# A pitch of 4128 bytes instead of 4096 for the 32 weight tiles of an attention and MoE kernel

## The chip, the core and the metric

The kernel runs on one core of a Trainium2 chip. The metric is the device time of one execution in microseconds (us): the median of the runs. A core has five engines that run side by side: TensorE (PE) multiplies matrices, VectorE (DVE), ScalarE (ACT) and GpSimd (POOL) work on elements, and SyncE (SP) issues the transfers (DMA) between the main memory and the core's own memory, SBUF. In SBUF a tile has 128 partitions, and in each of them it takes the same stretch of bytes. This document is about where that stretch begins.

## What is computed

Linear attention over 8 batches, 8 heads, 576 positions and 64 values a head, and behind it two matrix products with an activation between them:

```python
q_s = q - np.max(q, axis=-1, keepdims=True)
q_s = np.exp(q_s)
q_s = q_s / (np.sum(q_s, axis=-1, keepdims=True) + 1e-09)
k_s = k - np.max(k, axis=2, keepdims=True)
k_s = np.exp(k_s)
k_s = k_s / (np.sum(k_s, axis=2, keepdims=True) + 1e-09)
kv = np.einsum('bhsd,bhse->bhde', k_s, v)
attn = np.einsum('bhsd,bhde->bhse', q_s, kv)

x = attn.transpose(0, 2, 1, 3).reshape(4608, 512)
h = x @ w_in            # w_in: 512 x 2048
g = h - np.tanh(h)
out = g @ w_out         # w_out: 2048 x 512
```

`q`, `k` and `v` arrive as 4-byte numbers. The two weights arrive as 8-byte numbers (`float64`), which the kernel must decode itself.

## The kernel before

**Tiling.** The 4608 rows of `x` are worked through in 9 chunks of 512 (`j`), the 2048 hidden columns in 16 pieces of 128 (`f`). A step (`j`, `f`) forms `ph`, the transposed product of one piece of `w_in` with one chunk, applies the activation, and two steps later adds that piece's part to the four outputs `po` of the chunk. For accuracy each operand is split into a high and a low part of 4 bytes (`xh` and `xl`, `gh` and `gl`, two halves of each weight), and three of the four partial products are formed.

**Matmuls.** In `h_mm` (L568) the weights `w_i` are the stationary operand: a piece of 128 columns is loaded into PE (LDWEIGHTS), and 512 columns of `xh` or `xl` stream past it, 12 times for a step. In `o_mm` (L651) it is the other way round: 128 columns of `gh` or `gl` are loaded, and the 512 columns of one half of `w_o` stream, 12 times for a step. The attention adds small matmuls: `pm`, `pb`, `pk`, `pt`, `px`. In `pk` (L323) the values stream, 65 columns for each head, out of the tile `v` or out of a tile called `spare_v`, which for the second batch lies in a weight tile's place.

**Weight tiles.** There are 16 `w_in` and 16 `w_out` pieces, and each has one place in SBUF for the whole run, by its tag (`wi0` to `wi15`, `wo0` to `wo15`) in the pool `wts`. First the raw 8-byte numbers are loaded there (`load_weight`, L135 and L140), 512 KB, in pieces of 1 KB (`w_in`) or 4 KB (`w_out`). Five operations decode them (`split_weight`): a clamp on DVE (L157), a scaling of the high words (L161) and of the low words (L164) on ACT, a shift on DVE (L168) into a tile `c` of another pool, and a cast on ACT (L175). The cast writes the high half back to the same place, and a subtraction on POOL or DVE (L179) the low half. A few of the places hold something else before their weight comes: `wo15` a `q` tile, `wo13`, `wo14` and `wi14` transposed queries, and `wi15` the values of the second batch (`spare_v1`, L222), which need 4160 bytes.

**Places.** A pool hands out its places in the order in which tags are first asked for. A first pool, `lead`, fills SBUF up to a multiple of 256 bytes, and `LINE` and `line()` round sizes up to 256. A weight place is 4096 bytes in each partition, that of `wi15` is 4160 rounded up to 4352, and so every weight tile, and every other tile that is large (`xh`, `xl`, `g`, `gh`, `gl`, `u`, `t`, `mk`, `q`, `k`, `c`), begins at a multiple of 256. The small tiles and `v` stand in the last pool, `sm`, and begin at multiples of 32; `v` is at 192 modulo 256.

**Order.** The work up to step 19 is written out by hand in the table `ORDER`; from there the order on PE and SP is that of the code, and that on the other engines is found by a scheduler.

Of the kernel before, what the change touches and what calls it, by code (L numbers as in the profile page):

```python
# [10 lines left out]
F32 = mybir.dt.float32  # L11
F32R = mybir.dt.float32r
I32 = mybir.dt.int32
U32 = mybir.dt.uint32
I64 = mybir.dt.int64
# [55 lines left out]
def attn_moe_kernel(  # L71
# [10 lines left out]
    B, H, S, D = q.shape  # L82
    NT, DM = out.shape
    DFF = w_in.shape[1]
    P = 128
# [3 lines left out]
    NF = DFF // P  # L89
# [7 lines left out]
    def line(n: int) -> int:  # L97
        return -(-n // LINE) * LINE
# [4 lines left out]
    wts = ctx.enter_context(tc.tile_pool(name="wts", bufs=1))  # L103
# [24 lines left out]

    staged = {}
    wt = {}  # L130

    def load_weight(kind: str, f: int):
        w = wts.tile([P, DM], I64, name=f"raw_{kind}{f}", tag=f"w{kind}{f}")
        if kind == "i":
            nc.sync.dma_start(  # L135
                w.rearrange("p (c f) -> p c f", c=NC),
                w_in[:, f * P : (f + 1) * P].rearrange("(c p) f -> p c f", p=P),
            )
        else:
            nc.sync.dma_start(w, w_out[f * P : (f + 1) * P, :])  # L140
        staged[kind, f] = w

    def split_weight(kind: str, f: int) -> dict:

        st = {}

        def words(n: int) -> bass.AP:
            return staged[kind, f].bitcast(U32).rearrange("p (n t) -> p n t", t=2)[:, :, n]

        def clamp():
            hif = words(1).bitcast(F32)
            nc.vector.tensor_scalar(hif, hif, HI_MAX, -HI_MAX, op0=ALU.min, op1=ALU.max)  # L157

        def scale():
            hif = words(1).bitcast(F32)  # L160
            nc.scalar.activation(hif, hif, AF.Prelu, scale=2.0**-112, alpha=-(2.0**32))  # L161

        def low():
            nc.scalar.mul(words(0), words(0), 15.0 * 2.0**-33)  # L164

        def shift():
            st["c"] = c = dec.tile([P, DM], U32, name=f"c_{kind}{f}", tag="c")
            nc.vector.scalar_tensor_tensor(  # L168
                c, words(1), 3, words(0), op0=ALU.logical_shift_left, op1=ALU.bitwise_or
            )  # L170

        def cast():
            del staged[kind, f]
            wt[kind, f] = w = wts.tile([P, 2, DM], F32R, name=f"w_{kind}{f}", tag=f"w{kind}{f}")
            nc.scalar.copy(w[:, 0], st["c"].bitcast(F32))  # L175

        def rest(eng):
            w = wt[kind, f]
            eng.tensor_tensor(  # L179
                w[:, 1], st["c"].bitcast(F32), w[:, 0].bitcast(F32), op=ALU.subtract  # L180
            )

        return dict(cl=clamp, pr=scale, lo=low, st=shift, ca=cast, sub=rest)


# [28 lines left out]
    def v_ones(b: int, st: dict, u: int):  # L214

        if u < NKP:
            if b == 0 and u:
                vt = xp.tile([P, H, 2 * D + 2], F32, name="spare_v", tag="xh1")
            elif b == 1 and u:
                n = H * (2 * D + 2)  # L220
                vt = wts.tile([P, line(4 * n) // 4], F32, name="spare_v1", tag=f"wi{NF - 1}")
                vt = vt[:, :n].rearrange("p (h d) -> p h d", h=H)  # L222
            else:
                vt = sm.tile([P, H, 2 * D + 2], F32, name=f"v{b}_{u}", tag="v", bufs=1)
            nc.gpsimd.memset(vt[:, :, 0 :: 2 * D + 1], 1.0)
        else:
            vt = sm.tile([REST, H, D + 1], F32, name=f"vr{b}", tag="vr", bufs=1)
            nc.gpsimd.memset(vt[:, :, 0:1], 1.0)
        st["v", u] = vt
# [280 lines left out]
    def prepare(j: int, put):  # L510
# [6 lines left out]
        for b in new:  # L517
            st = {}
            for u in range(NKP + 1):
                put(0, lambda u=u: k_load(b, st, u))  # L520
            for u in (0, NKP):
                for part in (v_ones, v_load):
                    put(0, lambda u=u, part=part: part(b, st, u))
            for n in range(4):
                put(KX, lambda n=n: kv_max(b, st, n))
            for part in (kv_max_t, kv_row, kv_row_h, kv_row_l):
                put(KX + 2, lambda part=part: part(b, st))
            put(KX + 4, lambda: kv_rows(b, st))
            for u in range(NKP + 1):
                put(KX + 4, lambda u=u: kv_sub(b, st, u))  # L530
                put(KX + 4, lambda u=u: kv_exp(b, st, u))
            put(KX + 7, lambda: kv_mm(b, st, 0))
            for part in (v_ones, v_load):
                put(KX + 7, lambda part=part: part(b, st, 1))
            put(KX + 10, lambda: kv_mm(b, st, 1))
            put(KX + 10, lambda: kv_mm(b, st, NKP))
            for n in range(3):
                put(KX + 10, lambda n=n: kv_den(b, st, n))
            put(KX + 10, lambda: kv_norm(b, st))
# [169 lines left out]
    for b in range(2):  # L709
        st = {}  # L710
        for u in range(NKP + 1):
            ops[f"k{b}.{u}"] = lambda b=b, st=st, u=u: k_load(b, st, u)
            ops[f"vo{b}.{u}"] = lambda b=b, st=st, u=u: v_ones(b, st, u)
            ops[f"v{b}.{u}"] = lambda b=b, st=st, u=u: v_load(b, st, u)
            ops[f"ks{b}.{u}"] = lambda b=b, st=st, u=u: kv_sub(b, st, u)
            ops[f"ke{b}.{u}"] = lambda b=b, st=st, u=u: kv_exp(b, st, u)
            ops[f"pk{b}.{u}"] = lambda b=b, st=st, u=u: kv_mm(b, st, u)
        for n, part in enumerate("abcd"):
            ops[f"km{b}.{part}"] = lambda b=b, st=st, n=n: kv_max(b, st, n)
        for n, part in enumerate(("sl", "rs", "rc")):  # L720
            ops[f"{part}{b}"] = lambda b=b, st=st, n=n: kv_den(b, st, n)
        for part, fn in dict(
            pm=kv_max_t, mx=kv_row, mh=kv_row_h, ml=kv_row_l, pb=kv_rows, kn=kv_norm
        ).items():
            ops[f"{part}{b}"] = lambda b=b, st=st, fn=fn: fn(b, st)
# [13 lines left out]
    for kind, f in pieces:  # L739
        ops[f"ld.{kind}{f}"] = lambda kind=kind, f=f: load_weight(kind, f)  # L740
        for part, fn in split_weight(kind, f).items():
            ops[f"{part}.{kind}{f}"] = fn
# [11 lines left out]
    with tc.manual_schedule(engines={ENG.PE, ENG.DVE, ENG.Activation, ENG.Pool, ENG.SP}):  # L754
        for name in ORDER.split():
            eng = (nc.vector,) if name[-1] == "*" else ()
            name = name.rstrip("*")
# [74 lines left out]
```

## Time and profile before

| | before |
|---|---|
| median of 3 runs | 898.78 us |
| lowest and highest run | 897.59 and 899.41 us |
| span of the profiled execution | 896.5 us |
| PE busy, matmuls | 874.3 us, 5008 matmuls |
| DMA | 57.47 MB, mean 64 GB/s |

The profile covers one execution. Its span, 896.5 us, runs from the first to the last instruction on the core; the profile states no device time of its own for that execution, so the span is what the working is made against, and the median of the runs stands 2.3 us above it. In the rows, L568 is line 568 of the kernel, "out<-in" are tile names with the buffer numbers left out (so `v` is every `v` tile, and `spare_v` both of its kind), `x1152` is a count, and two times behind a bar are the group's busy time in us and the mean of one in ns, followed by the engine's idle time before the group and what ended most of it. Slices are 40 equal parts of the span, each digit the busy share in tenths.

### The profile page before, as it was taken

What the parts mean: (1) busy time and instruction counts of PE and PEld (TensorE: products, weight loads), DVE (VectorE), ACT (ScalarE), POOL (GpSimd) and SP (SyncE); (2) the same over time, 40 slices, a digit from 0 to 9 for tenths busy, and PEclk for the clock granted to TensorE, in tenths of its full rate; (3) what the DMA queues carried; (4) which work ended last, traced back from release to release, by engine and by line L of the source; (5) the groups of instructions that cost most, each with busy time, mean ns of one, the idle gap of its engine ahead of it and who ended that gap; (6) DMA issues with size and microseconds to landing.
All of it is one profiled execution on the core that took longest, in us unless ns stands there. A gap on an engine that the chain in (4) does not pass through costs nothing.

```text
span 896.5 us, 13174 instructions
## 1 busy us (share of the span) xinstructions
PE 874.3 (98%) x5008; PEld 716.2 (80%) x5008; DVE 613.3 (68%) x906; ACT 555.3 (62%) x967; POOL 289.2 (32%) x246
## 2 busy tenths in 40 slices
PE   6899989999999999999999999999999999999997
PEld 5677778888888888888888888888888888888886
DVE  7999988957686767667656765765865566454444
ACT  4899986656554656555646665556646566556553
POOL 4641112433244224332333332422433224212221
PEclk8999999999999999999999999999999999999999
DMA  9983301040223102300140011301100020001001
GB/s 293 315 307 119 123 1 42 24 133 9 83 71 103 28 3 81 107 24 1 48 130 4 21 47 37 106 1 48 48 24 1 1 71 12 1 1 48 1 1 47
DMA packets 79775, 57.47 MB, mean 64 GB/s; under 512 B 14688, under 2 KB 72032, under 8 KB 79712
## 3 DMA queue, kind: packets, MB, share of 16 engines
q1 hardware_dynamic: 79712, 56.63, 20.7%
q8 instruction: 39, 0.64, 0.3%
q14 instruction: 24, 0.20, 0.1%
HBM read 46.14 MB, written 10.49 MB: 63 GB/s over the span
## 4 chain that ended last, share of the span: by engine, by line
PE 82%; DVE 8%; ACT 5%; DMA 2%; issue 1%; SPq 1%; POOL 1%; DVEq 0%; ACTq 0%; POOLq 0%
PE po L651 39%; PE ph L568 38%; PE pk L323 2%; PE px L487 2%; PE pt L461 1%; DVE g L589 1%; DVE t L594 1%; DMA raw_i<-in_moe_w_in_dram 1%; ACT mk L583 1%; DVE g L597 1%; DVE c_o L168 1%; DVE g L602 1%; DVE gl L608 1%; ACT raw_o L164 1%; ACT raw_o L161 1%
## 5 line engine op out<-in xcount | busy, mean ns | idle before, releaser
L651 PE MATMUL po<-w_o,gh 128*128 128x512 f32 x1152 | 359.1, 393 | 0.3 <-DVE w_o L179 0.2
L568 PE MATMUL ph<-xh,w_i 128*128 128x512 f32 x1152 | 313.0, 394 | 3.1 <-DVE t L594 2.3
L608 POOL TENSOR_TENSOR gl<-g,gh 128x512 fp32r<-128x512 f32 x128 | 170.9, 1335 | 387.0 <-ACT gh L605 356.7
L651 PEld LDWEIGHTS po<-w_o,gh 128*128 128x128 f32 x1152 | 214.6, 188 | 47.4 <-issue 1.9
L568 PEld LDWEIGHTS ph<-xh,w_i 128*128 128x128 f32 x1152 | 213.9, 188 | 47.8 <-DVE t L594 2.8
L589 DVE SCALAR_TENSOR_TENSOR g<-u,ph 128x512 f32<-128x512 f32 x144 | 98.2, 682 | 208.4 <-ACT t L583 202.6
L651 PE MATMUL po<-w_o,gl 128*128 128x512 f32 x576 | 224.5, 390 | 0.3 <-DVE gl L608 0.3
L605 ACT CAST gh<-g 128x512 fp32r<-128x512 f32 x144 | 89.6, 622 | 172.4 <-DVE g L602 163.8
L568 PE MATMUL ph<-xl,w_i 128*128 128x512 f32 x576 | 155.0, 391 | 0.0
L583 ACT ACTIVATE u<-ph 128x512 f32<-128x512 f32 x144 | 86.1, 598 | 72.9 <-PE ph L568 72.4
L597 DVE SCALAR_TENSOR_TENSOR g<-vv,g 128x512 f32<-128x512 f32 x144 | 117.8, 818 | 18.5 <-ACT vv L583 8.0
L651 PEld LDWEIGHTS po<-w_o,gl 128*128 128x128 f32 x576 | 108.3, 188 | 23.7 <-DVE gl L608 0.7
L568 PEld LDWEIGHTS ph<-xl,w_i 128*128 128x128 f32 x576 | 108.1, 188 | 23.6 <-DVE xl L508 0.5
L602 DVE COPY_PREDICATED g<-mk,t 128x512 f32<-128x512 int32 x144 | 117.9, 819 | 3.3
L583 ACT ACTIVATE mk<-ph 128x512 int32<-128x512 f32 x144 | 86.4, 600 | 37.7 <-DVE g L589 35.5
L583 ACT ACTIVATE vv<-u,b_pa 128x512 f32<-128x512 f32 x144 | 104.8, 728 | 0.4 <-DVE g L597 0.3
L594 DVE TENSOR_TENSOR t<-ph,t 128x512 f32<-128x512 f32 x144 | 98.1, 681 | 6.4 <-ACT mk L583 5.6
L583 ACT ACTIVATE t<-ph 128x512 f32<-128x512 f32 x144 | 85.6, 594 | 3.0 <-DVE g L589 3.0
L413 POOL TENSOR_TENSOR q<-q,mq 128x1024 f32<-128x1024 f32 x14 | 28.4, 2026 | 49.1 <-DVE mq L408 47.3
L447 POOL TENSOR_TENSOR qn<-q,sq 128x512 f32<-128x512 f32 x30 | 34.6, 1155 | 25.5 <-PE pt L461 12.8
L408 DVE TENSOR_REDUCE mq<-q 128x16 f32<-128x1024 f32 x15 | 18.3, 1217 | 25.4 <-DMA q<-in_q_dram 25.4
L179 POOL TENSOR_TENSOR w_i<-c_i,w_i 128x512 fp32r<-128x512 f32 x12 | 18.3, 1528 | 39.2 <-ACT w_i L175 39.1
(94 smaller groups left out, 575.4 us busy)
## 6 DMA issues: line engine op xcount, KB each, us to landing
k<-in_k_dram SPq DMA_DIRECT2D x16, 512.0 KB, 5.5
raw_i<-in_moe_w_in_dram SPq DMA_DIRECT2D x16, 512.0 KB, 6.6
raw_o<-in_moe_w_out_dram SPq DMA_DIRECT2D x16, 512.0 KB, 9.2
q<-in_q_dram SPq DMA_DIRECT2D x15, 512.0 KB, 3.9
v<-in_v_dram SPq DMA_DIRECT2D x14, 512.0 KB, 5.1
out_dram<-o SPq DMA_DIRECT2D x28, 256.0 KB, 2.4
kr<-in_k_dram SPq DMA_DIRECT2D x8, 128.0 KB, 5.2
spare_v<-in_v_dram SPq DMA_DIRECT2D x2, 512.0 KB, 8.5
```

Of the source, the lines that this page charges most:

```text
L179: eng.tensor_tensor(w[:, 1], st["c"].bitcast(F32), w[:, 0].bitcast(F32), op=ALU.subtract)
L413: eng.tensor_tensor(qf, qf, mq, op=ALU.subtract)
L447: eng.tensor_tensor(qn.rearrange("p a g d -> p g a d"), qt[:, :, j].rearrange("p (g a) d -> p g a d", g=2), sq[:, :, j : j + 1] .broadcast ...
L568: nc.tensor.matmul(ph, w[:, i, c], x[:, c, :], start=(n == 0), stop=(n == len(ops) - 1))
L583: nc.scalar.activation(new(tag, **of), st[src], fn, **kw)
L589: nc.vector.scalar_tensor_tensor(new("g"), st["u"], C2, st["ph"], op0=ALU.mult, op1=ALU.mult)
L594: nc.vector.tensor_tensor(st["t"], st["ph"], st["t"], op=ALU.subtract)
L597: nc.vector.scalar_tensor_tensor(st["g"], st["vv"], PB, st["g"], op0=ALU.add, op1=ALU.mult)
L602: nc.vector.copy_predicated(st["g"], st["mk"], st["t"])
L605: nc.scalar.copy(new("gh", F32R), st["g"])
L608: eng.tensor_tensor(new("gl", F32R), st["g"], st["gh"].bitcast(F32), op=ALU.subtract)
L651: nc.tensor.matmul(po[t], g[:, cols], wt["o", f][:, w], start=(begin and n == 0), stop=(end and n == 2),)
```

## The change

The weight places get a pitch of 4128 bytes (`PITCH`): a raw tile and a decoded tile are asked for with 32 bytes more than they use, and the code works on a view of the first 4096. The rounding of `spare_v1` to a multiple of 256 goes, so its place, `wi15`, is 4160 bytes. A tile `pad` of 224 bytes, which nothing reads or writes, is put ahead of the weights, and with it the pool again ends at a multiple of 256.

```diff
+    PITCH = 2 * DM * 4 + 32
+    taken = (2 * NF - 1) * PITCH + 4 * H * (2 * D + 2)
+    wts.tile([P, line(taken) - taken], mybir.dt.uint8, name="pad")
 
     def load_weight(kind: str, f: int):
-        w = wts.tile([P, DM], I64, name=f"raw_{kind}{f}", tag=f"w{kind}{f}")
+        w = wts.tile([P, PITCH // 8], I64, name=f"raw_{kind}{f}", tag=f"w{kind}{f}")[:, :DM]
...
         def cast():
             del staged[kind, f]
-            wt[kind, f] = w = wts.tile([P, 2, DM], F32R, name=f"w_{kind}{f}", tag=f"w{kind}{f}")
+            w = wts.tile([P, PITCH // 4], F32R, name=f"w_{kind}{f}", tag=f"w{kind}{f}")
+            wt[kind, f] = w = w[:, : 2 * DM].rearrange("p (t n) -> p t n", t=2)
...
                 n = H * (2 * D + 2)
-                vt = wts.tile([P, line(4 * n) // 4], F32, name="spare_v1", tag=f"wi{NF - 1}")
+                vt = wts.tile([P, n], F32, name="spare_v1", tag=f"wi{NF - 1}")
```

The instructions, their order on every engine and their waits are the same in both programs. What differs is the byte at which each weight tile begins in a partition. Before it is 0 modulo 256 for all; with the change, in the order of the places:

| start modulo 256 | tiles |
|---|---|
| 0 | `wi4`, `wo1`, `wo3`, `wo9` |
| 32 | `wi2`, `wi6`, `wo14`, `wo7` |
| 64 | `wo15`, `wi7`, `wo5`, `wi9` |
| 96 | `wi1`, `wo2`, `wo4`, `wi13` |
| 128 | `wo13`, `wi15`, `wo10`, `wo8` |
| 160 | `wi3`, `wi12`, `wi11` |
| 192 | `wi5`, `wi10`, `wo6`, `wi8` |
| 224 | `wi0`, `wo0`, `wi14`, `wo12`, `wo11` |

The second half of each decoded tile, and each piece of 128 columns in it, begins a multiple of 512 bytes behind the tile's start, so it has the same place modulo 256. The pool is 1024 bytes longer in all, and the tiles of the later pools stand 1024 bytes higher.

## Prediction

> **What bounds the kernel now.** I read the page's busy times and slices first, then the table of stretches, the costliest groups, and pieces of the timeline.
>
> ```profile
> PE 874.3 (98%) x5008; PEld 716.2 (80%) x5008; DVE 613.3 (68%) x906; ACT 555.3 (62%) x967; POOL 289.2 (32%) x246
> PE   6899989999999999999999999999999999999997
> DVE  7999988957686767667656765765865566454444
> PEclk8999999999999999999999999999999999999999
> DMA  9983301040223102300140011301100020001001
> ```
>
> TensorE (PE) is short of full only in the first slices, where VectorE (DVE) and the DMA rows are full. The table of stretches (busy us and instructions of each engine, granted clock, DMA share, GB/s) dates the change of hands:
>
> ```profile
> 0.00:27.00 27.00, 17.10 (x211) 16.24 (x215) 21.02 (x33) 15.06 (x22) 13.07 (x23) 0.87 0.93 267
> 27.00:44.00 17.00, 14.85 (x96) 12.08 (x87) 16.93 (x28) 14.21 (x26) 11.79 (x8) 1.00 1.08 358
> 70.00:100.00 30.00, 28.66 (x148) 22.36 (x147) 28.29 (x49) 28.39 (x54) 2.81 (x3) 1.00 0.32 114
> 176.00:300.00 124.00, 123.87 (x786) 100.81 (x785) 84.80 (x125) 70.95 (x123) 44.20 (x39) 1.00 0.26 77
> 300.00:600.00 300.00, 300.00 (x1727) 245.81 (x1727) 202.24 (x288) 177.44 (x308) 101.22 (x86) 1.00 0.16 45
> 800.00:884.00 84.00, 84.00 (x373) 69.56 (x372) 41.78 (x61) 46.55 (x81) 20.18 (x16) 1.00 0.04 13
> ```
>
> Three stages with different limits are in it. Up to 27 us the kernel is fed by its first loads (DMA share 0.93). Around 70 to 100 us DVE and ScalarE (ACT) are both over 28 of 30 us busy, since they decode weights beside the activation work. From 176 us on PE is busy for 123.87 of 124 us, 300 of 300 and 84 of 84, with at least a third of DVE idle: there the time is the number of matmuls times the pace of one. The pace is read from the timeline of the quietest piece (start, length from first start to last end, merged count):
>
> ```profile
> 804.65 1.07 PE L568 MATMUL ph<-xh,w_i 128*128 128x512 f32 x4
> 805.56 1.07 PE L568 MATMUL ph<-xl,w_i 128*128 128x512 f32 x4
> 806.47 1.07 PE L568 MATMUL ph<-xh,w_i 128*128 128x512 f32 x4
> 807.37 0.61 PE L651 MATMUL po<-w_o,gh 128*128 128x512 f32 x2
> 810.09 1.07 PE L568 MATMUL ph<-xh,w_i 128*128 128x512 f32 x4
> ```
>
> Twelve `ph` matmuls take 807.37 - 804.65 = 2.72 us, and the twelve `po` behind them 810.09 - 807.37 = 2.72 us, so 226.7 ns each, whichever operand is the weight. A matmul that becomes 1 ns slower is 1 ns longer in the total; nothing covers it. That is the sensitive place.
>
> **The change, part by part.** No instruction is added, removed or moved: the two programs agree on every engine, wait for wait, and only addresses differ. So the sum has no term for counts, only for what a new start address does to an instruction or transfer that touches a weight tile. In before, each of the 32 tiles starts at a multiple of 256 bytes. In the change the first starts at 224 modulo 256 and each next 32 further (64 further behind `wi15`, whose slot is 4160). Four tiles, `wi4`, `wo1`, `wo3` and `wo9`, land on multiples of 256; 15 of the `w_i` and 13 of the `w_o` do not. All other large tiles move up by 1024 bytes and keep their place modulo 256; I take that as nothing.
>
> *Matmuls that stream w_o (L651).* Each tile feeds 9 chunks of 4 outputs with 3 matmuls, 108 in all, so 13 x 108 = 1404 matmuls stream 512 columns from a start off 256. The rows:
>
> ```profile
> L651 PE MATMUL po<-w_o,gh 128*128 128x512 f32 x1152 | 359.1, 393 | 0.3 <-DVE w_o L179 0.2
> L651 PE MATMUL po<-w_o,gl 128*128 128x512 f32 x576 | 224.5, 390 | 0.3 <-DVE gl L608 0.3
> ```
>
> No 512-column matmul of this trace has an operand off 256, so the price is bounded by neighbours. The `pk` matmuls stream 65 columns out of `v`, which starts at 192 modulo 256, or out of `spare_v`, which starts at 0; the `pt` ones read only aligned operands:
>
> ```profile
> 53.67 1.15 PE L323 MATMUL pk<-spare_v,k 128*64 128x65 f32 x32
> 350.40 1.15 PE L323 MATMUL pk<-v,k 128*64 128x65 f32 x32
> 306.18 0.60 PE L461 MATMUL pt<-ident,qn 128*128 128x128 f32 x4
> L323 PE MATMUL pk<-v,k 128*64 128x65 f32 x448 | 16.1, 225 | 0.9 <-ACT k L312 0.9
> L461 PE MATMUL pt<-ident,qn 128*128 128x128 f32 x144 | 21.9, 276 | 0.0
> ```
>
> Both `pk` groups take 1.15 us: a start at 192 costs what a start at 0 costs. That is the lower end, 0 ns. It is weaker than it looks, because a head's 65 columns start another 520 bytes on, so both groups hold starts that are no multiple of 16. The upper end compares with `pt`: (0.60 - 0.276) / 3 = 108 ns for 128 columns, 0.84 ns a column. The 32 `pk` come as 16 steps of two (the halves of the output's partitions), (1.15 - 0.225) / 15 = 61.7 ns a step, against 65 x 0.84 = 54.8. If all of the difference were the crooked start, it would be 6.9 ns a matmul; part of it must be a step's fixed cost. So 0 to 6.9 ns on 1404 matmuls, 0 to 9.7 us. Below nothing a bound is only the whole excess of the 512-column pace over the `pt` pace at half the time a column, 226.7 - 512 x 0.42 = 11.7 ns, and no row shows that an aligned start causes it. I take 0, the end with the directly compared rows, and keep the rest for the rivals.
>
> *Weight loads of w_i (L568).* 15 x 108 = 1620 loads read 128 columns from off 256.
>
> ```profile
> L568 PEld LDWEIGHTS ph<-xh,w_i 128*128 128x128 f32 x1152 | 213.9, 188 | 47.8 <-DVE t L594 2.8
> ```
>
> A load takes 188 of the 226.7 ns; 47.8 us over 1152 is 41 ns of idle time before each. A load up to about 39 ns longer stays beside the matmul that streams meanwhile, if the stream sets the pace: 0. If instead the loop from load to matmul to next load sets it, each ns of the load counts, and the upper end is 1620 x 6.9 ns = 11.2 us.
>
> *Decode (L157 to L179).* 28 tiles off 256 pass 2 DVE and 3 ACT steps, 56 and 84 instructions, and then one subtraction, mostly in the DVE- and ACT-bound stretch. Nearest rows, one operation on `v` at 192 and on `spare_v` at 0 (min/median/max ns):
>
> ```profile
> L225 POOL MEMSET v<- x14: 112/119/121, 10.2 to 638.7; 128x16 f32 x14
> L225 POOL MEMSET spare_v<- x2: 116/118/119, 0.9 to 35.0; 128x16 f32 x2
> ```
>
> One ns apart; 84 x 1 ns is 0.1 us. I take 0.
>
> *Transfers into the tiles.* Here the trace does show a price. `q` and `v` are equal loads of 512 KB in pieces of 512 bytes, `q` to multiples of 256, `v` to rows of 520 bytes whose data begin 4 bytes in. The line under each issue is its time to landing:
>
> ```profile
> L235 SPq DMA_DIRECT2D v<-in_v_dram x14: 368/396/1258, 10.3 to 638.9; - x14
> DMA to landing us min/median/max: 4.0/5.1/9.2
> L393 SPq DMA_DIRECT2D q<-in_q_dram x15: 368/391/773, 0.7 to 721.6; - x15
> DMA to landing us min/median/max: 3.7/3.9/7.0
> ```
>
> The undisturbed (shortest) one costs 0.3 us more. Per weight transfer I bound the price by 0 and 0.3 us; the pieces are longer (1 KB and 4 KB), so less is likelier. What waits for weights is short:
>
> ```profile
> ACT raw_i L164 <- DMA raw_i<-in_moe_w_in_dram: 1.3, 1, 1.3
> PEld pk L323 <- DMA raw_i<-in_moe_w_in_dram: 0.4, 1, 0.4
> ```
>
> Two waits in the whole run. Everything else is covered by the decode's own backlog on DVE and ACT; without that cover, 28 transfers x 0.3 us would be 8.4 us. So two late landings at most, 0 to 0.6 us; I take 0.1, as the first wait is for `wi4`, itself on a multiple of 256, with one early transfer ahead of it.
>
> [...]
>
> **Sum.** 896.5 us of span + 0 + 0 + 0 + 0.1 = 896.6 us. The median of the runs, 898.78, is 2.3 us over the profiled span, for what lies around it and between executions; carried over, 898.9 us. A measurement of this kernel can tell about 0.2% (1.8 us) from no change, and this is within it.
>
> **Rivals.**
>
> *The crooked stream costs PE time (slower).* [...] At the upper price of 6.9 ns it is 9.7 us, 908.6 us; with the loads on the loop as well, 11.2 more, 919.8. It decides from 1.8 us / 1404 = 1.3 ns a matmul, which is not much beside a pace of 226.7, and PE has no slack from 176 us on. For it speak that lack of slack and that no row tests a 512-column stream; against it the two equal `pk` groups. At half the price, which I think likeliest if it happens, 903.7 us. Chance 0.36.
>
> [...]
>
> *Transfers late at the start (slower).* The 0.3 us of `v` against `q`, on the eight or so loads up to 30 us where the DMA share is about 1, pushes the first weights back by 8 x 0.3 = 2.4 us: 901.2 us. For it the share and 358 GB/s; against it two waits of 1.3 and 0.4 us. Chance 0.05.
>
> *Equal starts collide today (faster).* If the stream and the load beside it hinder each other because both start at 0 modulo 256, spreading the weights gives back up to 11.7 ns in 1404 + 1620 matmuls, 35 us: 863 us. Against it: the `pk` pace is the same with `v` at 192 and at 0. Chance 0.06.
>
> *The change does not do what it says.* The built addresses are as described, so this has no chance of its own.
>
> **How the numbers follow.** Forecast 0.53, slow PE stream 0.36, late transfers 0.05, collisions 0.06. So faster by over 0.2% is 0.06, within it 0.53, slower 0.41. The range leaves out the collisions (0.06) below and, of the slow stream, what costs more than 6 ns a matmul or takes the loads with it (about 0.1) above: 1404 x 6 ns = 8.4 us gives 907.3. Below, 0.2% under the median is 897.0. The forecast's own range is 897.0 to 900.6.
>
> **What would show it.** The timeline's pace of twelve `ph` and of twelve `po` should stay 2.72 us for all tiles. If the stream costs, `po` of `wo15` (64), `wo13` (128) or `wo6` (192) is longer than that of `wo1`, `wo3` and `wo9` in the same trace, and `ph` is not. If the loads are on the loop, `ph` is longer for all tiles but `wi4`, and LDWEIGHTS rises above 188 ns. Late transfers show as a longer wait of ACT L164 and a later first `ph`, with the pace unchanged. I am wrong if 2.72 has become 2.74 or more.

## The result, and the profile after

The change makes the kernel slower: 911.65 us median (911.27 to 913.99) against 898.34 us for before on the same occasions, a ratio of 1.0153 with a 95% interval of 1.0139 to 1.0168. The profiled span went from 896.5 to 909.6 us, by 13.1. The time lies above the range of the prediction, 897.0 to 907.3 us. Ratios compare undisturbed executions; one of the ten of experiment 1, at 3093 us, is left out of its ratio.

The page after, the rows that answer to those of before:

```profile
PE 890.9 (98%) x5008; PEld 718.1 (79%) x5008; DVE 611.3 (67%) x906; ACT 555.7 (61%) x967; POOL 292.4 (32%) x246
PE   6899999999999999999999999999999999999997
PEclk8999999999999999999999999999999999999999
DMA  9983301040314011300140011301100020001001
```

The counts are the same, and so are the granted clock (the row PEclk) and the busy times of DVE and ACT, to within 2 us. PE's busy time grew by 16.6 us, that of POOL, which is far from full, by 3.2. The table of stretches (same columns as before) says where:

```profile
70.00:100.00 30.00, 28.87 (x148) 22.29 (x147) 28.25 (x49) 28.37 (x55) 2.61 (x3) 1.00 0.32 112
176.00:300.00 124.00, 124.00 (x778) 99.22 (x777) 82.69 (x123) 69.83 (x121) 43.96 (x38) 1.00 0.27 77
300.00:600.00 300.00, 300.00 (x1703) 241.59 (x1703) 196.23 (x281) 174.32 (x302) 100.42 (x85) 1.00 0.16 45
```

Up to 100 us PE gets as many matmuls done as before (148 in the stretch from 70 to 100 us, then and now), while DVE and ACT are busy for over 28 of those 30 us. From 176 us on it gets fewer done in the same time, with no idle time between them: 778 for 786, 1703 for 1727. So it is the pace of the matmuls, and the loss grows evenly from there to the end. The timeline of PE, the place that answers to the prediction's (start, length, count):

```profile
821.15 1.10 PE L572 MATMUL ph<-xh,w_i 128*128 128x512 f32 x4
822.09 1.09 PE L572 MATMUL ph<-xl,w_i 128*128 128x512 f32 x4
823.02 1.09 PE L572 MATMUL ph<-xh,w_i 128*128 128x512 f32 x4
823.96 0.63 PE L655 MATMUL po<-w_o,gh 128*128 128x512 f32 x2
...
826.75 1.09 PE L572 MATMUL ph<-xh,w_i 128*128 128x512 f32 x4
...
829.55 0.62 PE L655 MATMUL po<-w_o,gh 128*128 128x512 f32 x2
...
832.29 1.07 PE L572 MATMUL ph<-xh,w_i 128*128 128x512 f32 x4
...
835.01 0.63 PE L655 MATMUL po<-w_o,gh 128*128 128x512 f32 x2
```

This is chunk 8. The twelve `ph` of `wi2` (32 modulo 256) take 823.96 - 821.15 = 2.81 us and the twelve `po` of `wo0` (224) take 2.79, where before both took 2.72. The twelve `po` at 829.55 are those of `wo1`, which starts at 0 modulo 256: 2.74. The twelve `ph` at 832.29 are those of `wi4`, also at 0: 2.72. So within one trace tiles off 256 are slow and tiles on it are not, and this holds alike for `ph`, where the weight is loaded, and for `po`, where it streams.

All starts of the change, from 176 us on, taken from the trace: the mean interval in ns from one matmul's start to the next, over the fifth to eleventh of each twelve, by the weight tile's start modulo 256.

| | 0 | 32 | 64 | 96 | 128 | 160 | 192 | 224 |
|---|---|---|---|---|---|---|---|---|
| `ph`, the weight is loaded | 226.7 | 233.2 | 233.3 | 234.3 | 233.6 | 233.5 | 229.4 | 233.3 |
| `po`, the weight streams | 228.5 | 232.8 | 232.8 | 233.5 | 233.4 | no tile | 233.6 | 233.3 |

Only a start at 0 keeps the pace; 128 is as bad as 32, so being alike modulo 128 is not enough. Modulo 256 is: in before, tiles stand at odd and even multiples of 256 (the place of `wi15` is 17 times 256 bytes), and the median of every one is 227 or 228 ns, over the eighth to eleventh matmul. (The 228.5 holds matmuls that had not yet settled, of which experiments 2 and 3 tell.)

A load itself did not become longer; LDWEIGHTS still takes 188 ns:

```profile
L572 PEld LDWEIGHTS ph<-xh,w_i 128*128 128x128 f32 x1152 | 213.9, 188 | 52.0 <-DVE t L598 2.3
```

### The profile page after: what moved, and what is told of

It is laid out like the page before. It is cut to its first block, busy times and chain, and to the rows that moved or that the text cites. A ratio compares the mean times of both kernels' runs of the same rounds, so it can differ in the third digit from the quotient of the medians.

```text
span 909.6 us, 13174 instructions
## 1 busy us (share of the span) xinstructions
PE 890.9 (98%) x5008; PEld 718.1 (79%) x5008; DVE 611.3 (67%) x906; ACT 555.7 (61%) x967; POOL 292.4 (32%) x246
## 4 chain that ended last, share of the span: by engine, by line
PE 86%; DVE 8%; ACT 4%; issue 1%; DMA 0%; POOL 0%; DVEq 0%; ACTq 0%
PE po L655 40%; PE ph L572 39%; PE pk L327 2%; PE px L491 2%; PE pt L465 1%; DVE g L593 1%; DVE t L598 1%; ACT mk L587 1%; DVE c_o L171 1%; DVE gl L612 1%; DVE c_i L171 1%; ACT raw_o L167 1%; DVE k L313 1%; ACT raw_o L164 1%; PE pm L263 0%
## 5 line engine op out<-in xcount | busy, mean ns | idle before, releaser
L655 PE MATMUL po<-w_o,gh 128*128 128x512 f32 x1152 | 363.9, 397 | 0.2 <-DVE w_o L183 0.2
L572 PE MATMUL ph<-xh,w_i 128*128 128x512 f32 x1152 | 318.1, 398 | 2.4 <-DVE t L598 1.9
L655 PE MATMUL po<-w_o,gl 128*128 128x512 f32 x576 | 227.1, 394 | 0.0
L572 PE MATMUL ph<-xl,w_i 128*128 128x512 f32 x576 | 158.1, 396 | 0.0
L606 DVE COPY_PREDICATED g<-mk,t 128x512 f32<-128x512 int32 x144 | 115.0, 799 | 3.3
L451 POOL TENSOR_TENSOR qn<-q,sq 128x512 f32<-128x512 f32 x30 | 36.9, 1229 | 25.4 <-PE pt L465 12.7
```

Source lines behind the costliest of these rows:

```text
L451: eng.tensor_tensor(qn.rearrange("p a g d -> p g a d"), qt[:, :, j].rearrange("p (g a) d -> p g a d", g=2), sq[:, :, j : j + 1] .broadcast ...
L572: nc.tensor.matmul(ph, w[:, i, c], x[:, c, :], start=(n == 0), stop=(n == len(ops) - 1))
L606: nc.vector.copy_predicated(st["g"], st["mk"], st["t"])
L655: nc.tensor.matmul(po[t], g[:, cols], wt["o", f][:, w], start=(begin and n == 0), stop=(end and n == 2),)
```

## The experiments

Two theories came out of this. **LINE**: an operand that starts off a multiple of 256 costs a fixed price. **DIFFERENCE**: the place itself is free, and what costs is that the operand that streams and the operand that is loaded beside it start at different places modulo 256. In before all starts are 0, so the two can't be told apart there.

### 1 and 5: everything 32 bytes higher

```diff
-    lead.tile([P, line(nc.sbuf_base) - -(-nc.sbuf_base // 32) * 32], mybir.dt.uint8, name="lead")
+    lead.tile([P, line(nc.sbuf_base) - -(-nc.sbuf_base // 32) * 32 + 32], mybir.dt.uint8, name="lead")
```

> The kernel before with every large tile 32 bytes higher: all weights, activations and x tiles start at 32 modulo 256, so each is off a multiple of 256, but the operand that streams and the operand that is loaded meanwhile start at the same place modulo 256. Theory LINE (an operand that starts off a multiple of 256 costs a matmul about 6 ns, whichever operand it is): a pace of twelve matmuls of 2.80 us or more, and a time of at least 911 us. Theory DIFFERENCE (the price comes from a stream and a load that start at different places modulo 256): a pace of 2.72 us and 898 us.

900.46 us median of ten, ratio 1.0018 (1.0009 to 1.0028). The timeline is that of experiment 5, the same kernel in one more execution:

> The first experiment's kernel once more, for a profile of an undisturbed execution. DIFFERENCE: twelve ph and twelve po take 2.72 us each. LINE: 2.80 us.

It took 900.48 us. Its timeline:

```profile
817.71 1.07 PE L568 MATMUL ph<-xh,w_i 128*128 128x512 f32 x4
...
820.43 0.61 PE L651 MATMUL po<-w_o,gh 128*128 128x512 f32 x2
...
823.15 1.07 PE L568 MATMUL ph<-xh,w_i 128*128 128x512 f32 x4
```

2.72 us for `ph` and 2.72 us for `po`, though nothing large starts at a multiple of 256. LINE falls. What is left, 0.18%, is not pace. The span of experiment 5, 898.7 us, is 2.2 us over that of before, and the distance is there by 277 us (the `pk` group that stood at 350.40 in before stands at 352.58, and the rest keeps that distance). One part comes at the start: the first `ph` is at 31.1 us where before has it at 29.7, and the loads run at less than in before, whose second row is shown last:

```profile
27.00:44.00 17.00, 14.86 (x130) 12.62 (x131) 16.93 (x27) 13.57 (x25) 10.87 (x9) 0.93 1.05 329
44.00:70.00 26.00, 25.73 (x200) 20.72 (x201) 25.12 (x46) 24.22 (x45) 11.28 (x8) 0.98 0.94 316
...
44.00:70.00 26.00, 24.84 (x208) 19.51 (x208) 25.24 (x47) 24.29 (x45) 10.48 (x7) 1.00 0.80 279
```

From 27 to 44 us 329 GB/s are moved where before moved 358, and the DMA engines are busy longer behind (0.94 against 0.80). Here `q` and `k` too land off a multiple of 256, as well as the weights. In experiment 6, where `q` and `k` do and the weights do not, the first `ph` is at 31.3 us; in the change, where only the weights do, it is at 29.9. That fits a price for transfers to crooked places, as the prediction read it from `v` against `q`; it was not taken apart further. The lower granted clock is not the reason alone: experiment 4 has 0.91 from 27 to 44 us and its first `ph` at 29.9.

The other part comes between 205 and 277 us, where PE waits three times for POOL, 0.4 to 0.6 us each, as it does not in before; why is open. (In between, the trace of before itself loses 1.6 us at a granted clock of 0.96 from 135 to 176 us, so the parts do not simply add up to 2.2.)

### 2 and 3: only one kind of weight

The weights of the two kinds get a pool each, and only one of them the pitch of 4128 (that of `w_in` in experiment 2, as here, that of `w_out` in experiment 3):

```diff
+    wtso = ctx.enter_context(tc.tile_pool(name="wtso", bufs=1))
...
+    PITCH = {"i": 4128, "o": 4096}
+    POOL = {"i": wts, "o": wtso}
...
-        w = wts.tile([P, DM], I64, name=f"raw_{kind}{f}", tag=f"w{kind}{f}")
+        w = POOL[kind].tile([P, PITCH[kind] // 8], I64, name=f"raw_{kind}{f}", tag=f"w{kind}{f}")
+        w = w[:, :DM]
```

> Only the 16 w_in tiles at a pitch of 4128, the w_out tiles at multiples of 256. Both theories: the twelve ph take 2.80 us, the twelve po 2.72 us, and about half of the loss, 905 us. A theory in which only the stream of w_out pays gives 898 us; one in which a late weight transfer pays gives 902 us and no change of pace.

906.33 us, ratio 1.0085 (1.0070 to 1.0101).

> Only the 16 w_out tiles at a pitch of 4128, the w_in tiles at multiples of 256. Both theories: the twelve po take 2.80 us, the twelve ph 2.72 us, and about half of the loss, 905 us. A theory in which only the loads of w_in pay gives 898 us.

905.97 us, ratio 1.0084 (1.0062 to 1.0107). The two kinds cost the same, some 0.85% each. In the timeline of experiment 3 the twelve `po` from 819.15 take 2.82 us and the `ph` behind them 2.76:

```profile
819.15 0.63 PE L660 MATMUL po<-w_o,gh 128*128 128x512 f32 x2
...
821.97 1.09 PE L577 MATMUL ph<-xh,w_i 128*128 128x512 f32 x4
822.89 1.09 PE L577 MATMUL ph<-xl,w_i 128*128 128x512 f32 x4
823.82 1.07 PE L577 MATMUL ph<-xh,w_i 128*128 128x512 f32 x4
824.73 0.62 PE L660 MATMUL po<-w_o,gh 128*128 128x512 f32 x2
```

The `ph` here have all operands in their old places, and yet the first four last until 822.89 - 821.97 = 0.92 us, the next 0.93 and only the last 0.91 (227 ns each). The pace comes back some matmuls late. That would explain why the two halves add up to more (15.0 us by the medians) than the change (13.3): each also slows the start of the other kind's twelve. A price on the stream of w_out alone, on the loads of w_in alone, or on late transfers is out: both kinds lose, and in pace.

### 4: the 1024 bytes by themselves

```diff
+    wts.tile([P, 1024], mybir.dt.uint8, name="pad")
```

> The kernel before with 1024 unused bytes ahead of the weights: all large tiles from the weights on stand 1024 bytes higher, at multiples of 256 as before. Both theories: 2.72 us a twelve and 898 us. If the move of the later pools by 1024 bytes were a part of the loss, it would be above 900 us.

897.80 us, ratio 0.9988 (0.9978 to 0.9998): the higher place of the later pools is no part of the loss.

### 6: the other side moved

The weights at multiples of 256, and everything behind them 32 bytes higher:

```diff
+    xp.tile([P, 32], mybir.dt.uint8, name="pad")
```

> Weights and identity at multiples of 256, all pools behind them (x, g and the rest) 32 bytes higher: the weights are where before has them, and the other operand of every matmul starts 32 further modulo 256. DIFFERENCE: as bad as the change, 2.80 us a twelve for ph and for po, 911 to 913 us. A theory in which the weight tiles must start at multiples of 256: 898 us.

916.41 us, ratio 1.0202 (1.0185 to 1.0219), above the 911 to 913 expected. The weights were where before had them, and it is the slowest of the kernels with this order, since now nearly every 512-column matmul has a load beside it that starts elsewhere:

```profile
819.72 1.09 PE L569 MATMUL ph<-xh,w_i 128*128 128x512 f32 x4
...
822.52 0.63 PE L652 MATMUL po<-w_o,gh 128*128 128x512 f32 x2
...
825.32 1.09 PE L569 MATMUL ph<-xh,w_i 128*128 128x512 f32 x4
```

2.80 and 2.80 us. Weights at multiples of 256 are not enough. Part of the loss is not pace, since `q` and `k` land at crooked places here as in experiment 5.

### 7: two pairs

`x` and `w_in` at 32, `g` and `w_out` at 96 modulo 256:

```diff
+    for pool, n in ((wts, 32), (wtso, 64), (xp, 192), (gp, 64), (ap, 160)):
+        pool.tile([P, n], mybir.dt.uint8, name="pad", bufs=1)
```

> x and w_in tiles at 32 modulo 256, g and w_out tiles at 96: nothing is at a multiple of 256, and the tiles do not share one start, but within ph and within po the streamed and the loaded operand do. DIFFERENCE: 2.72 us a twelve except where a load of the one pair runs beside a stream of the other (2 of 24 matmuls), so at most 288 x 6 ns = 1.7 us, 898 to 901 us. LINE, or a theory in which all tiles must share one start: 2.80 us and 911 us.

903.47 us, ratio 1.0055 (1.0039 to 1.0072): far from the 911 of LINE, but above the 901 that DIFFERENCE allowed. The timeline shows the reason:

```profile
820.95 1.08 PE L574 MATMUL ph<-xh,w_i 128*128 128x512 f32 x4
821.87 1.07 PE L574 MATMUL ph<-xl,w_i 128*128 128x512 f32 x4
822.78 1.07 PE L574 MATMUL ph<-xh,w_i 128*128 128x512 f32 x4
823.68 0.62 PE L657 MATMUL po<-w_o,gh 128*128 128x512 f32 x2
...
826.44 1.08 PE L574 MATMUL ph<-xh,w_i 128*128 128x512 f32 x4
```

The twelve `ph` take 2.73 us: four in 0.92, then four in 0.91 and four in 0.90. The twelve `po` take 2.76. My bound counted 2 matmuls of 24 at 6 ns, 12 ns for each two twelves. It is 2.73 + 2.76 - 2 x 2.72 = 0.05 us, because one unequal load disturbs the matmuls behind it too; by the starts in the trace a `po` twelve runs at intervals between 224 and 236 ns until its eleventh. The same ragged intervals, 224 to 240 ns, stand in before behind the groups of small matmuls, mostly for seven to eleven matmuls.

### 8: halves at steps of 4 bytes

`FINE` holds (1, 5), (2, 6), (3, 7) and (4, 8), in words of 4 bytes.

```diff
-            wt[kind, f] = w = w[:, : 2 * DM].rearrange("p (t n) -> p t n", t=2)
+            o1, o2 = FINE[(f + (kind == "o")) % 4]
+            wt[kind, f] = w = (w[:, o1 : o1 + DM], w[:, DM + o2 : DM + o2 + DM])
```

> The change, with each half of each decoded weight 4 to 32 bytes further into its place, so that the halves start at 64 places modulo 256 that are multiples of 4. DIFFERENCE with a period of 256 bytes: no half is faster than 226.7 ns a matmul and nearly all are about 233, 911 to 913 us. If the stream and the load collide by place, a few bytes of lead could be better than none: some halves below 226 ns. If only whole 32 byte pieces matter, halves within 28 bytes of a multiple of 256 keep 226.7 ns.

909.80 us, ratio 1.0127 (1.0107 to 1.0147), a little under the 911 to 913 expected. Subtracting the starts of matmuls that follow each other in the trace and taking the mean for each half, most halves lie between 228 and 238 ns, and none under 226. Because the two halves of a tile alternate here, none had time to settle, so single values say little. No faster place showed, though a weak test like this one does not exclude it.

### 9 and 10: which two operands

While a matmul streams, PE loads the weights of the next one: in the trace of before, from 176 us on, that load starts 3 ns behind the start of the stream (median of 2794) and takes 188 of its 226.7 ns. In the runs so far that load had the same start as the matmul's own weights nearly always. Issuing one `ph` and one `po` in turn separates the two. From step 33 on, for both kernels:

```diff
+                mixed = n > 2 * NF
+                if mixed:
+                    beside += o_singles(*steps[n - LAG])
                 h_step(j, f)
...
             nc.tensor.matmul(
                 ph, w[:, i, c], x[:, c, :], start=(n == 0), stop=(n == len(ops) - 1)
             )
+            if beside:
+                beside.pop(0)()
```

`o_singles` gives the twelve `po` matmuls of a step one by one, and experiment 10 has `x` and `w_in` at 32 modulo 256 and `g` and `w_out` at 0.

> Control for the next one: the kernel before with, from step 33 on, the twelve ph of a step and the twelve po of the step two before issued in turn, one ph, one po, all large tiles at multiples of 256. BESIDE (what counts is the start of the operand loaded while another streams, that is, of the next matmul's weights) and OWN (what counts are the two operands of one matmul) alike: every interval starts equal, 226.7 ns in the undisturbed pieces, about 898 us.

> The same interleaved order with the x and w_in tiles at 32 modulo 256 and the g and w_out tiles at 0. Each matmul's own two operands start at the same place, but beside each stream the load for the other kind runs, which starts 32 away. BESIDE: intervals of about 233 ns and about 12 us more than the control. OWN: 226.7 ns and the time of the control.

The control is at 940.80 us, far over 898, because in this order PE waits more for the activation of a step (from 300 to 600 us it is busy 287.39 of 300 us); only its pace is used. Experiment 10 is at 950.66, ratios to before 1.0473 (1.0442 to 1.0503) and 1.0582 (1.0552 to 1.0613). The timeline of the control, then that of experiment 10:

```profile
860.78 0.39 PE L694 MATMUL po<-w_o,gh 128*128 128x512 f32 x1
861.00 0.39 PE L570 MATMUL ph<-xh,w_i 128*128 128x512 f32 x1
...
862.37 0.39 PE L570 MATMUL ph<-xl,w_i 128*128 128x512 f32 x1
862.59 0.39 PE L694 MATMUL po<-w_o,gh 128*128 128x512 f32 x1
```

```profile
871.04 0.39 PE L700 MATMUL po<-w_o,gl 128*128 128x512 f32 x1
871.27 0.40 PE L576 MATMUL ph<-xh,w_i 128*128 128x512 f32 x1
...
872.67 0.39 PE L576 MATMUL ph<-xh,w_i 128*128 128x512 f32 x1
872.90 0.39 PE L700 MATMUL po<-w_o,gh 128*128 128x512 f32 x1
```

Eight matmuls take 862.59 - 860.78 = 1.81 us in the control, 226 ns each, and 872.90 - 871.04 = 1.86 us in experiment 10, 233 ns each. Every matmul of experiment 10 has its own two operands at equal starts; only the load that runs beside each stream starts 32 away. So OWN falls. The loss, 9.9 us, is near the 12 expected.

One rival remains in this order: the next stream, too, starts 32 away. Experiment 2 separates it. Its `x`, `g` and `w_out` are all at 0, so the last `po` of a twelve has equal operands of its own and is followed by a stream from 0; only the load beside it, of the next `w_in` tile, can start elsewhere. In the twelves from 300 us on that had settled at 226 to 227 ns, that last interval is 235 ns every time (16 of 16) when the next tile starts at 32 (`wi0`, `wi8`, `wi15`), and 226 to 227 (7 of 7) when it starts at 0 (`wi7`, `wi11`). At 160 and 224 it is 235 to 237, at 128 it is 232 to 233, at 96 it is 228 to 229; at 64 and 192 it stays at 225 to 226, and the price comes with the matmuls behind. The reverse holds in experiment 3: there the last `ph` of a settled twelve is followed by a `w_out` stream that mostly starts elsewhere, its load is equal, and it takes 225 to 228 ns. So BESIDE holds: what counts is the next matmul's weights against this matmul's stream.

### 11 and 12: how equal is equal

The `x` tiles alone are moved by a few bytes within a longer place (`LATER` is 1 and 63 words for the even and the odd place, in experiment 12 it is 4 and 60):

```diff
-                xp.tile([P, NC, CH], F32R, name=f"x{p}{j}", tag=f"x{p}{place}") for p in "hl"
+                xp.tile([P, NC * CH + 64], F32R, name=f"x{p}{j}", tag=f"x{p}{place}")[
+                    :, o : o + NC * CH
+                ].rearrange("p (c n) -> p c n", c=NC)
+                for p in "hl"
```

> The kernel before with the x tiles moved, the weights at multiples of 256: in chunks 0, 3, 5 and 7 x starts 4 bytes past a multiple of 256, in chunks 1, 2, 4, 6 and 8 it starts 4 bytes ahead of one. po is left as before. If the two starts must be exactly equal: twelve ph take about 2.80 us in both kinds of chunk and the time is about 905 us. If what counts is the same piece of 16 or 32 bytes: 2.72 us with x 4 past, 2.80 us with x 4 ahead, and about 902 us.

> The same with 16 bytes past (chunks 0, 3, 5, 7) and 16 bytes ahead (chunks 1, 2, 4, 6, 8). Exactly equal or same piece of 16: 2.80 us in both, 905 us. Same piece of 32: 2.72 us with x 16 past, 2.80 us with x 16 ahead, 902 us. No theory gives a pace under 2.72 us; if one shows, it is a version to build on.

907.50 us, ratio 1.0102 (1.0072 to 1.0132), and 906.89, ratio 1.0095 (1.0064 to 1.0127). The timeline of experiment 11, a twelve of chunk 7 (4 bytes past) and one of chunk 8 (4 ahead); then that of experiment 12, chunk 7 (16 past) and chunk 8 (16 ahead):

```profile
765.77 1.12 PE L575 MATMUL ph<-xh,w_i 128*128 128x512 f32 x4
...
768.63 0.62 PE L658 MATMUL po<-w_o,gh 128*128 128x512 f32 x2
...
823.51 1.08 PE L575 MATMUL ph<-xh,w_i 128*128 128x512 f32 x4
...
826.27 0.39 PE L658 MATMUL po<-w_o,gh 128*128 128x512 f32 x1
```

```profile
764.83 1.09 PE L575 MATMUL ph<-xh,w_i 128*128 128x512 f32 x4
...
767.61 0.62 PE L658 MATMUL po<-w_o,gh 128*128 128x512 f32 x2
...
816.78 1.10 PE L575 MATMUL ph<-xh,w_i 128*128 128x512 f32 x4
...
819.58 0.61 PE L658 MATMUL po<-w_o,gh 128*128 128x512 f32 x2
```

2.86 us with `x` 4 bytes past, 2.76 with it 4 bytes ahead, 2.78 with 16 past, 2.80 with 16 ahead; 2.72 is the equal case. (The means of all undisturbed twelves from 176 us on, 28 to 41 of each kind, are the same to 0.01 us.) None of the four is free, so no piece of 16 or 32 bytes forgives a difference, and 4 bytes past cost most: 2.86 - 2.72 over twelve is 11.7 ns a matmul. Both times lie above the expected 902 and 905, since I had one price for all unequal starts, and it depends on the difference and on its sign.

No kernel of the study clearly beats before; experiment 4 is 0.12% under it, less than the 0.2% that the prediction counts as no change.

## Why the prediction was wrong

**What bounds the kernel** held: the slower pace costs little at first (at 126 us the trace of the change stands 0.6 us behind that of before), and from 176 us on each ns of the pace is in the time.

**The matmuls that stream w_o** are the step that failed. I bounded their price between 0 and 6.9 ns and took 0, from the two equal `pk` groups. What the runs showed in place of 0 is (826.75 - 823.96) / 12 - 226.7 = 5.8 ns for `wo0`, near the upper end. The `pk` rows could not show it. Both groups hold starts 520 bytes apart against loads at multiples of 256, so both were nearly all unequal cases, and their agreement says nothing of an equal one. I had written that the comparison was weaker than it looked and used it all the same; the `pt` row, with equal starts throughout, was the only one with the case that was left behind. That the 6.9 ns from it come near the 5.8 measured may be partly luck, since a fixed cost of a `pk` step can be in them too, which no run separates.

**The weight loads**, also taken as 0, fail by another error. I asked only what a longer load would cost. It did not become longer: 188 ns before and after. But a `ph` took longer by about as much as a `po`, 7.5 ns for `wi2`, because the stream beside the load is what is held up. Twice 0.85% in experiments 2 and 3 shows that this half was as large as the other. The rival that I named, a slow stream at half the price and without the loads, was too small for both reasons: 903.7 us. Its upper case, with the loads, gave 919.8 us, above the measurement.

**The sum by the measured terms.** In the trace, the mean interval between 512-column matmuls that follow each other (leaving out those over 260 ns) went from 227.5 to 232.2 ns. It is not 226.7 to 233 because four tiles stay equal, because the `w_i` tiles at 192 cost only about 3 ns, and because the ragged intervals behind small matmuls were there before. From 176 us on there are 2797 such intervals in before, and at 4.76 ns each they make 13.3 us, beside the 13.1 of the two spans. The 505 ahead of 176 us would make 2.3 more, but there DVE and ACT set much of the time, and the trace of before has its stretch at a clock of 0.96: at 179 us the change stands 0.4 us ahead.

**Decode and transfers** went as predicted in what they cost, which is nothing that shows. The low-word scaling of `raw_i` has a median of 680 ns against 682, and its clamp 423 against 422, and the two waits for weights are the same to the tenth, though the median `w_in` load landed after 7.1 us where before has 6.6:

```profile
ACT raw_i L167 <- DMA raw_i<-in_moe_w_in_dram: 1.3, 1, 1.3
PEld pk L327 <- DMA raw_i<-in_moe_w_in_dram: 0.4, 1, 0.4
```

The start of experiment 5, 329 against 358 GB/s from 27 to 44 us, agrees in sign with the 0.3 us that I read from `v` against `q`; the change itself moved 357 GB/s in that stretch, and what its transfers cost stayed under the cover.

**The rivals.** The crooked stream had the sign right and the mechanism wrong: a crooked start costs no pace by itself (experiment 5, 2.72 us a twelve). That equal starts collide and unequal ones help had the mechanism of the pair right, stream and load, and the sign wrong. Its 11.7 ns were my estimate, from a column at half the `pt` time, 0.42 of 0.84 ns; what the runs showed at equal starts is 226.7 / 512 = 0.44 ns.

## What to carry to other kernels

When PE is the bound, look at where the streamed tile of one matmul and the weight tile of the next begin in their partition: here they had to be equal modulo 256 bytes, to the last 4, for the full pace, and a padding by 32 bytes cost 2 to 3% of most 512-column matmuls (227.5 to 232.2 ns on the mean of all, 226.7 to about 233 ns at the settled pace). The tiles may stand elsewhere as long as partners stand at the same place (all at 32 in experiment 5, 32 and 96 for the two pairs in experiment 7), so it is the common alignment that is worth keeping, and not a particular multiple. A row that serves as a bound must hold the case that is left behind as well as the one that is entered: two rows that are both in the new case agree whatever it costs.

## What the runs showed of the hardware that was not expected

A load slows the stream that runs beside it when the two start at different places, while the load itself keeps its 188 ns (the change, experiment 10): 226.7 ns a matmul at equal starts (experiment 5), 229 to 238 at others (the change, experiments 6, 10, 11, 12). Starts 16 bytes apart cost 5 to 7 ns a matmul (experiment 12), so the multiples of 16 that the prediction measured the `pk` starts by are no border.

After a disturbance the pace comes back by itself at equal starts, but only after up to ten matmuls or so of 224 to 240 ns (experiment 7, and before behind its small matmuls).

Why it is so stays open, and so does why the sign of a difference of 4 bytes is worth 2.86 against 2.76 us a twelve. The difference of the two starts alone does not fix the price either: with the weight 192 ahead of the stream it is about 3 ns, with the stream 64 ahead of the weight, the same modulo 256, about 6 (the table of the change).
